# A spectral mixer and a gated unit on one core: the opening written out as one list of pieces, and scales from exponents and norms

## The chip, the cores and the metric

One NeuronCore of a Trainium2 chip. The time is the device time of one execution in microseconds; three executions of the kernel before gave 475.52, 474.89 and 474.98, median 474.98 us.

## The reference, cut to what matters

```python
def reference(A_x, A_w_r, A_w_i, B_x, B_W_gate, B_W_up, B_W_down):
    x = A_x                                   # 1 x 2048 x 448, float32
    xn = _layernorm(x, axis=-1)
    X = rfft2(xn, axes=(-2, -1)) * (A_w_r + 1j * A_w_i)
    a = irfft2(X, s=(2048, 448), axes=(-2, -1))
    gate, up = xn @ B_W_gate, xn @ B_W_up     # 448 x 1792 each
    b = ((gate * (gate > 0)) * up) @ B_W_down # 1792 x 448
    return x + a + b
```

## The kernel before, in words

The gated unit is done in float16 with every operand split in a high half and a low half (high = the value rounded to float16, low = the rest), so a product is three passes: high times high, high times low, low times high. Weights are first multiplied by a power of two so that the halves fit float16; these scales are found on the chip.

**Tiles.** x has 16 tiles n2 = 0..15 of 128 rows by 448. They form four chunks q = n2 mod 4, taken in the order `CHUNKS` = 0, 2, 1, 3; chunk 0 is the tiles 0, 4, 8, 12 and chunk 2 the tiles 2, 6, 10, 14. A chunk's normalized rows, transposed, are the tile `T` (`T_62` is chunk 0, `T_63` chunk 2). The 14 blocks of 128 columns of the gate and up weights are f = 0..13, in groups of 5, 5 and 4. The weights of one f come as two slabs `wst` of 256 KB, g = 0 (gate) and g = 1 (up).

**Units.** One unit is a pair (f, q): 20 matmuls of 512 columns into PSUM `gu` (`gu_full`, L653), 10 for each g, and its share of the half passes (`gu_half`, L660): a set of four matmuls of 64 rows that serves two units at once, the pair in `mates`. It closes one unit and opens the next. `gu` has two buffers. Then `gu_post` (L685 to L689): relu on ScalarE, product on VectorE, high half `h` on ScalarE, low half on VectorE. After the units of a group and chunk come four down projections (`dn_mm`, L702), each of 3 passes per f, that need `h` and the split down weights `wdt`.

**Normalization of a tile.** `ln_stats` (VectorE, L217, L220), `ln_rstd` (a square root on ScalarE and six small VectorE operations, L229 to L235), `ln_xn` (L253 or L255), `ln_hi` (ScalarE, L262 or L264, followed by two small copies on POOL, L265 and L266), `ln_lo` (VectorE, L276 and L277). Chunk 0 is then transposed by TensorE into PSUM (`ln_tp`, L290) and copied to `T` (`ln_ev`, L296 and L298); the other chunks by DMA transposes (`ln_dma`, L284).

**Scales.** Of the gate and up weights: `w_sq` squares a slab on ScalarE with a running sum (L590), POOL sums over the partitions (L593), `w_scale` makes four small VectorE operations (L601 to L605), `w_hl` the high half on ScalarE (L612) and the low half on VectorE (L613). Of the down weights: `wd_max`, a maximum on VectorE for each f (L618) and a maximum over the partitions on POOL (L620). Of the filter: `wmax_red`, 16 maxima on VectorE (L422).

**Order.** Up to the first unit the order on TensorE, VectorE, ScalarE and SyncE (which issues the DMAs) is written out by hand inside `manual_schedule` (L913 to L982), with `NWARM` = 24 and later a few matmuls on the tile `warm` that compute nothing. From the second unit on, a loop over the units (L1019) emits a unit, the pieces that `sched` has put at it, and as much of the list `bg` (the work of the Fourier transforms and of later chunks) as its planned share of VectorE allows (`room`, `load`); a scheduler then places each instruction on its engine's queue. Every engine works its own queue in order.

Of the kernel before, what the change touches and what calls it, by code (L numbers as in the profile page):

```python
# [134 lines left out]
def tile_gfnet_reglu(ctx: ExitStack, tc: tile.TileContext, x, xr, wgu, wd, wf, ident, c_fd, c_fm, c_im, c_row, c_id,  # L135
# [88 lines left out]
    def ln_rstd(q, js=(0, 1, 2, 3)):  # L224
        n = len(js)
        w = ft([128, 6, 4], F32, "rs", 3)
        vv, r0, t, r, nm, sd = (w[:, i, 0:n] for i in range(6))
# [20 lines left out]
    def ln_xn(n2, act=True):  # L248
        xn_b[n2] = free.pop(0)
        xn[n2] = xn_b[n2].rearrange("p g c k -> p (g c k)")[:, 0:D]  # L250
        r, nm = rst[n2 % 4, n2 // 4]
# [4 lines left out]

    def ln_hi(n2, fused=False):
        t = tt[n2]
        o = t.rearrange("p a b -> p (a b)")[:, 0:D]
        r, nm = rst[n2 % 4, n2 // 4]  # L260
        if fused:
            A.activation(o, xr_t[n2], AF.Identity, scale=r, bias=nm)  # L262
        else:
# [4 lines left out]
    def ln_norm(n2):
        new_tt(n2)
        ln_xn(n2, False)  # L270
        ln_hi(n2)
        free.append(xr_b.pop(n2))
# [819 lines left out]
```

## Time and profile before

| | |
|---|---|
| median of three executions | 474.98 us |
| the profiled execution | 474.69 us |
| its span, first to last instruction | 472.9 us |
| TensorE busy | 457.6 us (97%), 2713 matmuls |
| VectorE busy | 391.4 us (83%) |
| ScalarE busy | 169.9 us (36%) |
| POOL busy | 34.5 us (7%) |

Busy time is a sum over stages. In a slice of the span, the granted clock of TensorE is given as a share of full speed; a matmul that runs at half the clock is just as busy. A timeline row gives the start, the time from the first start to the last end of the merged instructions, engine, line and operation, what it writes and reads, how many, and in brackets the idle time of the engine before it and whose end released it.

### The profile page before, as it was taken

What the parts mean: (1) busy time and instruction counts of PE and PEld (TensorE: products, weight loads), DVE (VectorE), ACT (ScalarE), POOL (GpSimd) and SP (SyncE); (2) the same over time, 40 slices, a digit from 0 to 9 for tenths busy, and PEclk for the clock granted to TensorE, in tenths of its full rate; (3) what the DMA queues carried; (4) which work ended last, traced back from release to release, by engine and by line L of the source; (5) the groups of instructions that cost most, each with busy time, mean ns of one, the idle gap of its engine ahead of it and who ended that gap; (6) DMA issues with size and microseconds to landing.
All of it is one profiled execution on the core that took longest, in us unless ns stands there. A gap on an engine that the chain in (4) does not pass through costs nothing.

```text
span 472.9 us, 7492 instructions
## 1 busy us (share of the span) xinstructions
PE 457.6 (97%) x2713; PEld 235.2 (50%) x2713; DVE 391.4 (83%) x952; ACT 169.9 (36%) x342; POOL 34.5 (7%) x68
## 2 busy tenths in 40 slices
PE   8578999999999999999999999999999999999996
PEld 4433455555455555544444444444455655655653
DVE  6779459787989799998999999997989978856652
ACT  5746224241434275232212133253254134244120
POOL 2104002000500021000000001100000000000000
PEclk9899999999999999999999999999999999999999
DMA  7999501601144524314111010010231201200212
GB/s 256 384 380 238 144 0 35 124 17 51 37 106 139 157 94 135 103 39 120 41 41 40 1 40 21 2 45 1 71 99 52 82 15 45 91 32 25 77 43 78
DMA packets 38397, 41.38 MB, mean 87 GB/s; under 512 B 16390, under 2 KB 34534, under 8 KB 38360
## 3 DMA queue, kind: packets, MB, share of 16 engines
q1 hardware_dynamic: 38360, 40.90, 28.3%
q8 instruction: 21, 0.34, 0.3%
q14 instruction: 16, 0.13, 0.1%
HBM read 30.34 MB, written 3.67 MB: 72 GB/s over the span
## 4 chain that ended last, share of the span: by engine, by line
PE 89%; DVE 3%; DMA 2%; POOL 1%; issue 1%; ACT 1%; SPq 1%; POOLq 0%; ACTq 0%
PE gu L653 48%; PE dn L702 26%; PE gu L660 3%; PE fx L569 3%; PE fx L310 3%; PE fx L541 2%; PE fx L349 2%; DMA wst<-in_wgu 2%; PE fx L351 1%; PE fx L353 1%; POOL tt L265 1%; DMA T<-tt 1%; ACT junk L590 1%; DVE wdm L618 0%; ACT wt L612 0%
## 5 line engine op out<-in xcount | busy, mean ns | idle before, releaser
L653 PE MATMUL gu<-T,wt 128*128 128x512 f16 (+1 forms) x1140 | 256.7, 377 | 5.1 <-DVE wsc L603 2.5
L653 PEld LDWEIGHTS <-wt 128*128 128x128 f16 x1140 | 110.3, 98 | 133.9 <-issue 12.3
L702 PE MATMUL dn<-wdt,h 128*128 128x448 f16 x672 | 135.0, 352 | 1.7 <-ACT wdt L639 0.9
L702 PEld LDWEIGHTS <-h 128*128 128x128 f16 x672 | 65.3, 98 | 62.7 <-issue 3.5
L685 ACT ACTIVATE g<-gu 128x512 f32<-128x512 f32 x56 | 33.2, 593 | 102.4 <-PE gu L660 61.9
L686 DVE SCALAR_TENSOR_TENSOR g<-gu,g 128x512 f32<-128x512 f32 x56 | 38.5, 688 | 29.6 <-ACT g L685 29.5
L688 ACT ACTIVATE h<-g 128x512 f16<-128x512 f32 x56 | 35.0, 625 | 35.8 <-DVE g L686 35.8
L689 DVE TENSOR_TENSOR h<-g,h 128x512 f16<-128x512 f32 x56 | 38.6, 689 | 8.5 <-ACT h L688 8.4
L708 DVE SCALAR_TENSOR_TENSOR xy<-dn,dsc,xy 128x448 f32<-128x448 f32 x48 | 32.3, 680 | 6.2 <-PE dn L702 5.9
L612 ACT ACTIVATE wt<-wst,wsc 128x512 f16<-128x512 f32 x28 | 18.8, 713 | 16.2 <-DVE wsc L604 16.2
L613 DVE SCALAR_TENSOR_TENSOR wt<-wst,wsc,wt 128x512 f16<-128x512 f32 x28 | 20.4, 751 | 2.4 <-ACT wt L612 2.4
L557 ACT ACTIVATE pgh<-pg 114x512 f16<-114x512 f32 x16 | 10.1, 628 | 33.8 <-DVE pg L555 24.7
L593 POOL PARTITION_ALL_REDUCE wm<-wm x15 | 10.2, 681 | 159.2 <-ACT junk L590 159.2
L660 PE MATMUL gu<-T,wt 64*128 64x512 f16 x112 | 17.0, 381 | 3.3 <-DVE wt L613 2.7
L590 ACT ACTIVATE junk<-wst 128x512 bf16<-128x512 f32 x28 | 17.5, 623 | 7.4 <-DMA wst<-in_wgu 7.2
L569 PE MATMUL fx<-idc_t,pgh 114*128 114x112 f16 (+1 forms) x192 | 16.4, 236 | 0.0
L525 ACT ACTIVATE vt<-y,fsc 128x456 f16<-128x456 f32 x16 | 10.7, 671 | 14.4 <-PE fx L541 10.0
L342 ACT ACTIVATE Xh<-X 128x456 f16<-128x456 f32 x16 | 9.2, 577 | 17.8 <-PE fx L353 9.7
L560 DVE TENSOR_TENSOR pgh<-pg,pgh 114x512 f16<-114x512 f32 x16 | 11.0, 690 | 4.8 <-ACT pgh L557 4.7
L452 ACT ACTIVATE wf<-wf 128x114 f32<-128x114 f32 x16 | 4.6, 294 | 27.2 <-DVE y L459 13.1
L310 PE MATMUL fx<-fd_t,T 128*128 128x114 f16 x192 | 14.2, 225 | 0.0
L363 DVE TENSOR_TENSOR y<-y,y 128x456 f32<-128x456 f32 x22 | 13.8, 629 | 0.3
(113 smaller groups left out, 481.5 us busy)
## 6 DMA issues: line engine op xcount, KB each, us to landing
wst<-in_wgu SPq DMA_DIRECT2D x28, 256.0 KB
wmx<-in_wf SPq DMA_DIRECT2D x16, 228.0 KB
wf<-in_wf SPq DMA_DIRECT2D x16, 228.0 KB
wf<-y SPq DMA_DIRECT2D x32, 112.2 KB
y<-in_xr SPq DMA_DIRECT2D x16, 224.0 KB
xy<-in_x SPq DMA_DIRECT2D x16, 224.0 KB
out<-xy SPq DMA_DIRECT2D x16, 224.0 KB
wdst<-in_wd SPq DMA_DIRECT2D x14, 224.0 KB
```

Of the source, the lines that this page charges most:

```text
L310: P.matmul(o, T[:, a, js], fd_t[:, fd_off[part]:fd_off[part] + (2 * GW if part in wide else GW)], start=first, stop=True, skip_group_check ...
L569: P.matmul(ps[:, o0:o1], h[:, a, i, :], idc_t[:, b, c0:c0 + o1 - o0], start=(j == 0 and i < 3), stop=True, skip_group_check=True)
L590: A.activation(mt([128, 512], BF16, "junk"), wst[f, g].rearrange("p a b -> p (a b)"), AF.Square, scale=SQ, accum_out=m[:, 0, g:g + 1])
L613: V.scalar_tensor_tensor(w[:, 4:8, :], st, sc, w[:, 0:4, :], op0=OP.mult, op1=OP.subtract)
L653: last["P"] = P.matmul(hps[f, q][:, g, cs], wt[f, g][:, a, :], Tq[q][:, b, cs], start=(start and i == 0), stop=(stop and i == len(seq) - 1 ...
L660: m = P.matmul(hps[f, q][:, g, 0:512], wt[f, g][rows, 7, :], Tq[q][rows, b, :], start=start, stop=not start).ins
L685: last["A"] = A.activation(g1, hps[f, q][:, 0, :], AF.Relu, scale=2.0 ** -22).ins
L686: last["V"] = V.scalar_tensor_tensor(g1, hps[f, q][:, 1, :], 2.0 ** -22, g1, op0=OP.mult, op1=OP.mult).ins
L688: A.activation(h[:, 0, :], g1, AF.Copy)
L689: V.tensor_tensor(h[:, 1, :], g1, h[:, 0, :], op=OP.subtract)
L702: last["P"] = P.matmul(ps[:, 0:D], ht[f, q][:, a, js], wdt[f][:, b, :], start=(i == 0), stop=(i == n - 1)).ins
L708: last["V"] = V.scalar_tensor_tensor(xy[:, n2, :], dps[n2][:, 0:D], dsc[:, g:g + 1], xy[:, n2, :], op0=OP.mult, op1=OP.add).ins
```

## The change

`OPENING` lists the pieces of the first five units (f = 0..4 of chunk 0), one name for each, and each engine takes its own in the order of the list; POOL is now among the engines whose order is written by hand. The list holds the loads (`lx` and `ly` are x, `lw` a slab, `lwd` the down weights, `lfd` the constant `fd_t`), the normalization of the chunks 0 and 2, the scales, the splits, the matmuls (`hh`, `lh`, `hl` the quarters of unit one; `gu1g0` and so on the slabs of the next units; `hp` the half passes), the relu, product and halves of the five units, and the split of the down weights of the first group. All other work is held behind the list's last instructions on VectorE, ScalarE and SyncE, and the loop over the units starts at the sixth. `kw` and `warm` are the matmuls that compute nothing, 19 and three sets of 1, 6 and 3.

Scales: the squares with a running sum are used for the down weights and the filter too (`squares`, on ScalarE), in place of the VectorE maxima; the power of two comes from the exponent bits of the sum of squares by two integer operations (`half_exponent`, `shift_exponent`), so `w_scale` has two VectorE operations instead of four, `wd_scale` ten instead of eight. `ln_rstd` has five or, for the chunks 2, 1 and 3, four operations; `ln_xn` is always on VectorE. The loads of x and of the filter move to later units; the filter's loads and squares are spread through the transforms of the chunks 2 and 1.

```diff
+OPENING = """
+lx0 lx4 lw lid lw lx8 lx12 lw lw lw lw lx2 lx10 lx6 lx14 lwd0 lwd1 lwd2 lwd3 lwd4 warm st0 st4 sqA rsA hi4
+xn4 xn0 wsqW0g0 cp4 st8 hi0 parW0g0 st12 wsqW0g1 cp0 tpA0 lo0 tpA4 kw1 wscW0g0 sqB tpB0 kw6 parW0g1 wsqW1g0
+rsB whiW0g0 vevB0 lo4 wsqW1g1 xn12 tpB4 kw3 hi8 parW1 wscW0g1 xn8 whiW0g1 cp8 vevA0 vevA4 hi12 tpA8 vevB4
+hh10 hh00 lo8 wsqW2g1 cp12 tpA12 hl00 lo12 aevA12 tpB8 aevA8 hl10 wloW0g0 lw aevB8 tpB12 wscW1 lh00 aevB12
+wloW0g1 lw lfd hh01 hh11 whiW1g0 st2 lh01 lh10 whiW1g1 hl01 wloW1g0 lw hl11 wsqW2g0 wloW1g1 lw ly0 ly4 ly8
+ly12 lh11 wsqW3g0 st10 parW2 hp0 st14 wsqW3g1 gu1g0 st6 wdq0 parW3 wscW2 sqC wscW3 whiW2g0 rsC gu1g1 re0
+wloW2g0 whiW3g1 tm0 whiW2g1 xn6 wsqW4g0 xn2 gu2g0 wloW2g1 hi2 re1 xn10 gh0 wloW3g1 whiW3g0 tm1 gu2g1 wdq1
+wloW3g0 hi10 xn14 lo2 hi14 hi6 cp14 hp2 wsqW4g1 cp2 lo6 gu3g0 cp10 dm2 lo14 re2 parW4 wdq2 cp6 wscW4 tm2
+whiW4g0 dm14 lo10 wdq4 gu3g1 wloW4g0 gh1 dm10 gl0 whiW4g1 gl1 dm6 gu4g0 re3 wloW4g1 wdq3 tm3 wdp gh3
+wdsc gh2 gu4g1 gl2 wdh1 wdh2 wdl1 wdh0 wdl2 hp4 gl3 re4 wdh3 tm4 wdl0 gh4 wdh4 gl4 wdl3 wdl4 lw lw lw
+lw lw lw
+"""
...
+    def squares(src, acc):
+        A.activation(mt([128, 512], BF16, "junk")[:, 0:src.shape[-1]], src, AF.Square, scale=SQ, accum_out=acc)
+
+    def half_exponent(e, s):
+        V.tensor_scalar(e.bitcast(U32), s.bitcast(U32), 1, EXPMASK, op0=OP.logical_shift_right, op1=OP.bitwise_and)
+
+    def shift_exponent(o, e, sign, n):
+
+        V.tensor_scalar(o.bitcast(U32), e.bitcast(U32), float(sign), n * EXPONE, op0=OP.mult, op1=OP.add)
...
-        V.tensor_scalar(sc[:, 0, 0:n], e, TINY * SQ * 2.0 ** -64, 2.0 ** 50 / SQ, op0=OP.max, op1=OP.mult)
-        V.reciprocal(sc[:, 1, 0:n], sc[:, 0, 0:n])
-        V.tensor_scalar(e, e, TINY * SQ * 2.0 ** -64, 2.0 ** 64 / SQ, op0=OP.max, op1=OP.mult)
+        half_exponent(e, state["wm", f][:, 1, gs[0]:gs[-1] + 1])
+        shift_exponent(sc[:, 0:len(gs)], e, -1, 188)
...
-            V.tensor_reduce(m[:, 0, i:i + 1], wdst[f], axis=AX.X, op=OP.max, apply_absolute_value=True)
+        squares(wdst[f], state["wdm"][:, 0, i:i + 1])
...
-        V.tensor_reduce(small[:, k2:k2 + 1], state["wmx", k2], axis=AX.XY, op=OP.max, apply_absolute_value=True)
+        squares(state["wsq", k2].rearrange("p a b -> p (a b)"), small[:, k2:k2 + 1])
...
     with tc.manual_schedule(engines={mybir.EngineType.PE, mybir.EngineType.DVE, mybir.EngineType.Activation,
-                                     mybir.EngineType.SP}):
+                                     mybir.EngineType.SP, mybir.EngineType.Pool}):
...
+        for name in OPENING.split():
+            pieces[name]()
+    state["opened"] = True
+    free.extend(xr_b.pop(n2) for n2 in list(xr_b))
+    for e in "SVA":
+        ctx.enter_context(tc.issue_after(last[e]))
...
-    for i, u in enumerate(units):
+    for i, u in list(enumerate(units))[len(groups[0]):]:
```

SyncE's queue behind the first eleven loads, before: x and the down weights stand ahead of most of the slabs (`wst`). `y` read from in_xr is x for the normalization, `xy` read from in_x is x for the sum at the end, `wdst` the down weights.

```order
L195 DMA wst<-in_wgu 128x512 x4
L183 DMA xy<-in_x 128x448 x4
L189 DMA y_74<-in_xr 128x448
L189 DMA y_75<-in_xr 128x448
L189 DMA y_76<-in_xr 128x448
L189 DMA y_77<-in_xr 128x448
L195 DMA wst<-in_wgu 128x512
L205 DMA wdst<-in_wd 128x448 x5
L988 DMA fd_t<-in_c_fd 128x1710
L183 DMA xy<-in_x 128x448 x4
L209 DMA fm<-in_c_fm 128x768 x2
L195 DMA wst<-in_wgu 128x512
```

The same place in the changed kernel:

```order
L226 DMA wst<-in_wgu 128x512 x4
L220 DMA y_70<-in_xr 128x448
L220 DMA y_71<-in_xr 128x448
L220 DMA y_72<-in_xr 128x448
L220 DMA y_73<-in_xr 128x448
L236 DMA wdst<-in_wd 128x448 x5
L226 DMA wst<-in_wgu 128x512 x2
L976 DMA fd_t<-in_c_fd 128x1710
L226 DMA wst<-in_wgu 128x512 x2
L214 DMA xy<-in_x 128x448 x4
L319 DMA_TRANSPOSE T_63<-tt_97 128x8x128
```

The four slabs of the units four and five stand ahead of all loads of `xy`, and the transposes of chunk 2 right behind these.

POOL's queue from the fill of `warm`, before. `ISA` without operands configures POOL, `ISA wm<-wm` is the sum over the partitions, the copies are those of `ln_hi` for the x tiles `tt`:

```order
L925 MEMSET warm 128x512
L593 ISA
L593 ISA wm<-wm 128x1
L265 COPY tt_97<-tt_97 128x48
L266 COPY tt_97<-tt_97 128x64
L265 COPY tt_98<-tt_98 128x48
L266 COPY tt_98<-tt_98 128x64
L593 ISA wm<-wm 128x1
```

And in the changed kernel:

```order
L1031 MEMSET warm 128x512
L299 COPY tt_97<-tt_97 128x48
L300 COPY tt_97<-tt_97 128x64
L193 ISA
L193 ISA wm<-wm 128x1
L299 COPY tt_98<-tt_98 128x48
L300 COPY tt_98<-tt_98 128x64
L193 ISA wm<-wm 128x1
L193 ISA wm<-wm 128x2
```

The two copies of the first tile moved ahead of the configuring instruction.

VectorE's queue from the first normalization to the first low halves, before:

```order
L255 TENSOR_SCALAR y_70<-y_66,rs 128x448
L601 TENSOR_SCALAR eg<-wm 128x1
L603 TENSOR_SCALAR wsc<-eg 128x1
L604 RECIPROCAL wsc<-wsc 128x1
L605 TENSOR_SCALAR eg<-eg 128x1
L255 TENSOR_SCALAR y_71<-y_67,rs 128x448
L613 SCALAR_TENSOR_TENSOR wt<-wst,wsc,wt 128x512
L276 TENSOR_TENSOR tt_97<-y_70,tt_97 128x384
L277 TENSOR_TENSOR tt_97<-y_70,tt_97 128x64
L217 BN_STATS bst<-y_68 128x6
L220 BN_AGGR mv<-bst 128x2
```

And in the changed kernel:

```order
L286 TENSOR_SCALAR y_74<-y_67,mv,rs 128x448
L286 TENSOR_SCALAR y_75<-y_66,mv,rs 128x448
L248 BN_STATS bst<-y_68 128x6
L251 BN_AGGR mv<-bst 128x2
L248 BN_STATS bst<-y_69 128x6
L251 BN_AGGR mv<-bst 128x2
L310 TENSOR_TENSOR tt_98<-y_75,tt_98 128x384
L311 TENSOR_TENSOR tt_98<-y_75,tt_98 128x64
L196 TENSOR_SCALAR eg<-wm 128x1
L200 TENSOR_SCALAR wsc<-eg 128x1
L264 RECIPROCAL rs<-rs 128x2
```

Both statistics of the third and fourth tile moved ahead of the first scale, and the low half of the weights (`wt`) moved behind the low halves of all four tiles.

## Rows read from the trace of the kernel before

**Rows 1.** Busy time by stretch: stretch, length, TensorE, weight loads, VectorE, ScalarE, POOL, clock, DMA.
```profile
1.49:10.73 9.24, 9.09 (x35) 3.73 (x36) 6.43 (x22) 4.74 (x11) 1.77 (x5) 1.00 0.90 279
10.73:24.22 13.49, 8.55 (x70) 6.20 (x69) 10.19 (x35) 10.01 (x22) 2.68 (x7) 0.87 1.05 386
24.22:50.29 26.07, 21.67 (x105) 9.26 (x103) 21.89 (x64) 13.92 (x28) 6.39 (x11) 1.00 0.98 298
50.29:459.81 409.52, 409.48 (x2465) 211.74 (x2464) 348.84 (x825) 139.61 (x281) 22.71 (x36) 1.00 0.21 61
```

**Rows 2.** Timeline of TensorE in the first 51 us.
```profile
19.79 3.96 PE L653 MATMUL gu<-T,wt 128*128 128x256 f16 x20 [2.50 <-DVE wsc L603]
...
24.22 8.81 PE L653 MATMUL gu<-T,wt 128*128 128x512 f16 x40
35.75 0.61 PE L660 MATMUL gu<-T,wt 64*128 64x512 f16 x4 [2.72 <-DVE wt L613]
...
46.71 2.43 PE L702 MATMUL dn<-wdt,h 128*128 128x448 f16 x12 [0.23 <-DVE wdt L640]
49.75 0.61 PE L660 MATMUL gu<-T,wt 64*128 64x512 f16 x4 [0.61 <-DMA T<-tt]
```

**Rows 3.** The chain that ended last: start, length, what.
```profile
28.02 4.79 DMA wst<-in_wgu
...
57.81 4.32 PE gu L653 x20
...
200.75 5.67 PE dn L702 x30
```

**Rows 4.** VectorE: timeline rows, then groups by form (busy us, mean ns, idle before).
```profile
22.22 1.42 DVE L613 SCALAR_TENSOR_TENSOR wt<-wst,wsc,wt 128x512 f16<-128x512 f32 x2 [0.42 <-ACT wt L612]
...
37.03 1.35 DVE L255 TENSOR_SCALAR y<-y,rs 128x448 f32<-128x448 f32 x3
...
41.38 0.56 DVE L276 TENSOR_TENSOR tt<-y,tt 128x384 f16<-128x384 f32 x1
...
41.99 0.56 DVE L276 TENSOR_TENSOR tt<-y,tt 128x384 f16<-128x384 f32 x1
...
L422 DVE TENSOR_REDUCE small<-wmx 128x1 f32<-128x456 f32 x16 | 9.9, 626 | 3.8 <-DMA wmx<-in_wf 3.6
L217 DVE BATCH_NORM_STATS2 bst<-y 128x6 f32<-128x448 f32 x16 | 9.4, 617 | 2.5 <-DMA y<-in_xr 2.5
...
L234 DVE SCALAR_TENSOR_TENSOR rs<-rs 128x2 f32<-128x2 f32 x2 | 0.3, 161 | 0.1
```

**Rows 5.** ScalarE: two timeline rows, then the squares by form.
```profile
9.59 1.09 ACT L296 ACTIVATE T<-fx 128x384 f16<-128x384 f16 x2 [0.95 <-PE fx L290]
...
19.64 1.32 ACT L612 ACTIVATE wt<-wst,wsc 128x512 f16<-128x512 f32 x2
...
L590 ACT ACTIVATE junk<-wst 128x512 bf16<-128x512 f32 x28 | 17.5, 623 | 7.4 <-DMA wst<-in_wgu 7.2
...
L590 ACT ACTIVATION_READ_ACCUMULATOR junk<-wst 128x1 f32 x28 | 5.3, 188 | 0.0
```

**Rows 6.** Timeline of POOL: the first sum, copies of two x tiles.
```profile
6.30 0.53 POOL L593 PARTITION_ALL_REDUCE wm<-wm  x1 [4.87 <-ACT junk L590]
7.11 0.22 POOL L265 COPY tt<-tt 128x48 f16<-128x48 f16 x1 [0.27 <-ACT tt L262]
...
40.16 2.60 POOL L265 COPY tt<-tt 128x48 f16<-128x48 f16 x1
...
42.71 1.40 POOL L266 COPY tt<-tt 128x64 f16<-128x64 f16 x1
```

**Rows 7.** The transposes of chunk 2: SyncE's issue (timeline), transfer (chain).
```profile
41.63 6.06 SPq L284 DMA_TRANSPOSE T<-tt  x4
...
46.43 3.19 DMA T<-tt
```

More of the change, by code (lines that the diff above doesn't have):

```diff
@@ L268, in ln_norm @@
     def ln_norm(n2):
[L269 to L270 removed]
+        ln_xn(n2)
         ln_hi(n2)
+        ln_copy(n2)
         free.append(xr_b.pop(n2))
@@ L660, in gu_half @@
         m = P.matmul(hps[f, q][:, g, 0:512], wt[f, g][rows, 7, :], Tq[q][rows, b, :], start=start, stop=not start).ins
-        tc.add_manual_dep(m, prev.name, NOSYNC, reason="half passes stand together")
+        if "opened" in state:
+            tc.add_manual_dep(m, prev.name, NOSYNC, reason="half passes stand together")
         return m
@@ L726, in ln_chunk @@
     def ln_chunk(q):
-        if q != CHUNKS[1]:
-            for j in range(4):
-                add(0.0, load_xr, q + 4 * j)
+        for j in range(4):
+            add(0.0, load_xr, q + 4 * j)
         for j in range(4):
             add(0.79, ln_stats, q, j)
-        add(1.0, ln_rstd, q)
+        add(0.0, ln_sd, q)
+        add(0.7, ln_rstd, q)
         n = [q + 4 * j for j in (0, 2, 1, 3)]
@@ L752, in fft_chunk @@
                     add(0.0, load_fm, n[i])
+            k = state.get("wk", 0)
+            if q != CHUNKS[0] and k < 16:
+                if k > 1:
+                    add(0.0, wsq, k - 2)
+                add(0.0, wsq_load, k)
+                state["wk"] = k + 1
         for par in range(2):
@@ L767, in tile_gfnet_reglu @@
     fft_chunk(1)
-    for k in range(16):
-        add(0.0, wmax, k)
-        if k >= 2:
-            add(0.62, wmax_red, k - 2)
-    add(0.62, wmax_red, 14)
-    add(0.62, wmax_red, 15)
-    add(0.1, wmax_fin)
+    for k in (14, 15):
+        add(0.0, wsq, k)
+    add(0.1, wsq_fin)
     fft_chunk(3)
-    add(0.3, wmax_scale)
+    add(0.8, wsq_scale)
     add(0.0, open_inv)
@@ L978, in tile_gfnet_reglu @@
-        w_hl(1, 0)
-        w_hl(1, 1)
-        gu_full(0, 0, (1,), half[1], False, False, seq1 + seq2)
-        for j in range(4):
-            load_xr(CHUNKS[1] + 4 * j)
-    ctx.enter_context(tc.issue_after(last["V"]))
-    for _ in range(4):
-        load_wn()
-    for f in groups[0]:
-        load_wd(f)
-    nc.sync.dma_start(fd_t, c_fd)
+        gu_open(0, q)
+        for name in OPENING.split():
+            pieces[name]()
+    state["opened"] = True
+    free.extend(xr_b.pop(n2) for n2 in list(xr_b))
```

316 lines of the change are left out of this document (161 added, 155 removed).

## The prediction

> **What bounds the kernel now.** I read the busy time by stretch first, then TensorE's own timeline of the first 51 us, then what fed it there. From 50.29 to 459.81 us TensorE is busy 409.48 of 409.52 us [rows 1]: nothing that happens in that stretch on another engine shortens the run, as long as it stays off TensorE's path. VectorE is at 348.84 of 409.52 us there, so it is close behind, but it is behind. What is not filled lies in front: from 10.73 to 24.22 us TensorE has 8.55 us of 13.49 and from 24.22 to 50.29 us 21.67 of 26.07 [rows 1]. The timeline says where: 2.50 us of idle before the row at 19.79, 2.72 us before 35.75, 0.61 us before 49.75, and smaller ones around the first down passes at 46 us [rows 2]. The row at 19.79 is also slow: 20 narrow matmuls in 3.96 us, in a stretch with a granted clock of 0.87 [rows 1, 2]. Behind the wait at 35.75 stands a weight transfer of 4.79 us in the chain [rows 3], in a stretch in which the DMA engines are busy at 0.98 to 1.05 of their time [rows 1]; behind 49.75 the transposes of the second chunk [rows 7].
>
> **The frame of the sum.** After 50.29 us (the end of the half passes that close unit five and open unit six) the work of TensorE is the same list in both kernels. Before, 14 passes of the first down projection had been done by then (the 12 at 46.71 us and two just ahead of them [rows 2]); the new list ends with these half passes and does all down passes behind them. One pass is 5.67 / 30 = 0.189 us [rows 3], 14 are 2.65 us. So with H for the moment at which the half passes of unit five end,
> span after = H + (472.90 - 50.29) + 2.65 = H + 425.3.
> H in the terms of the kernel before is 50.29 - 2.65 = 47.6. The profiled execution took 474.69 us, 1.79 more than its span, and lies 0.29 under the median 474.98; I add both.
>
> **H, part by part: up to unit two.** The queue that is full first is VectorE's. The third and fourth tile of x are behind 1.47 MB of issued transfers, the same in both; before, 279 GB/s moved from 1.49 to 10.73 us, that is 2.58 MB, and then 386 GB/s [rows 1], so 1.47 MB is there about (2.58 - 1.47) / 0.386 = 2.9 us before 10.73: near 8 us. From 8.1 VectorE's list up to the second low half of unit one is: two statistics at 0.62 and a small operation of 0.16 each, 1.5; four low halves of x at the step of 0.61 from 41.38 to 41.99 [rows 4], 2.4; three scales of two small operations and one set of five, at 0.16 each or 0.2 with the hand-over [rows 4], 2.0; two normalizations at 1.35 / 3 = 0.45, 0.9; four copies out of PSUM, of 384 and 640 columns, for which I take 0.3 and 0.45 by their width against the 512 of a low half, 1.5; two low halves of weights at 1.42 / 2 = 0.71, 1.4 [rows 4]. Sum 9.7: it ends at 17.8. On the way, after the copy that frees the second PSUM buffer of the transposes (8.1 plus 6.8 of the above = 14.9), TensorE does six transposes and six narrow matmuls to 16.3; ScalarE then copies four T parts (0.49 to 0.7 each by 1.09 / 2 and width, 2.5 with a wait of 0.3 for the last transposes), makes two high halves of weights at 0.66 [rows 5], VectorE the low half, 0.75. That is 16.3 + 0.3 + 2.5 + 1.3 + 0.8 = 21.2, and the first half passes end at 21.8. Before they end at 24.22 [rows 2]: **2.4 us**.
>
> **Units two to five.** They hold 80 matmuls of 4.32 / 20 = 0.216 us [rows 3] and one more set of half passes, 50.29 - 49.75 = 0.54 us [rows 2]: 17.8 us, so 39.6 without a wait. Before, 26.07 us went there, 2.65 of them down passes; 4.40 us were idle [rows 1]. The waits go because of the transfers: the four slabs of units four and five come behind four tiles of x and wd alone (and fd_t between them), no longer behind twelve more tiles of x, fm and the x of a third chunk; each is issued when a low half frees its buffer, over 5 us ahead of its use. Five VectorE maxima of wd become ScalarE squares at 0.62 + 0.19 [rows 5]. What is late next is ScalarE: between 20.4 and 37 us its list has six high halves of weights (4.0), five squares of weights (3.8), four of wd (2.9), four high halves of x, three relus and two h copies (nine at 0.5 to 0.62, by width, 5.0), 15.7 of 16.6 us. So it is nearly full, and the last high half of weights is ready about when TensorE wants it. The last half passes need all four DMA transposes: before, four took 6.06 us of issue, some 1.4 apart, and the last landed at 46.43 + 3.19 = 49.6 [rows 7]. The new order can issue the first at 33 us, when the POOL copies are through, the last at 37; landing 3 us later, 40.2. **H = 40.2 + 0.6 = 40.8** if no operation slips. Two queues at 90% and more with in-order hand-overs don't run without a slip; I put 1.0 us on it, from the waits of 0.23 to 0.61 us that the same hand-overs show [rows 2]. H = 41.8, span 467.1, time 467.1 + 1.79 + 0.29 = **469.2 us**, 5.8 less than before (1.2%).
>
> **Edits that cost nothing here.** Sixteen maxima of the filter on VectorE at 0.626 [rows 4] become ScalarE squares; nine more wd maxima; scales of four operations become two; one operation less in each normalization set. That is some 18 us of VectorE after the opening; TensorE's 409.48 of 409.52 covers it all, so I count 0. The cover is TensorE itself: if it stood still for VectorE anywhere, part of it would count. ScalarE gets 25 x 0.81 = 20 us more on 139.61 us of 409.52 [rows 1]: it stays under half.
>
> **Where row and skill differ.** POOL's configuring instruction (the ISA row without operands) stood behind the memsets, its first use (6.30) waits 4.87 us for ScalarE [rows 6], so whatever it loads is hidden in at most these 4.87 us. In the new order it stands behind the first two copies, which end near 7.5, and its first use is wanted at 7.8. Its price lies between 0 and 4.87 us; I take a small one, since POOL starts its first use as soon as ScalarE is done. The Trainium skill, "GPSIMD Engine Reference", section 2.1 "Instruction dispatch", says that the first call to a freshly loaded kernel pays a load of about 6 us that no profile row shows. The row of 6.30 speaks against the full figure, since less time lay there; by the page's own 6 us H would be some 3.8 us later and the time 473.0.
>
> **Rivals.**
> 1. *The load of POOL comes out of cover.* With all of 4.87 us the first all-reduce is ready at 7.5 + 4.87 + 0.53 = 12.9; VectorE reaches the scale that needs it at 8.1 + 1.5 + 0.6 = 10.2 and stands 2.7 us, with everything queued behind it. Time 471.9. For it: no row shows the load. Against: nothing says it is as long as its cover. 0.11.
> 2. *The clock falls again.* Before, after the thin stretch to 19.79 us, 20 narrow matmuls and four half passes took 24.22 - 19.79 = 4.4 us, against 20 x 0.11 (half of 0.216) + 0.54 = 2.7 [rows 2, 3]. The new list has 10 extra matmuls on warm in the gaps up to 14 us and TensorE still waits some 3 us there. +1.7: 470.9. 0.08.
> 3. *POOL's copies of the second chunk starve.* Two copies take 0.22 each when free [rows 6], but 2.60 and 1.40 at 40.16, where VectorE runs two-input operations back to back [rows 4, 6]. I counted 0.9 per pair; three pairs stand in POOL's queue ahead of the sum for unit five's weights. At 2.0 per pair H is 3.3 later: 472.5. The Trainium skill, same page, section 8 "Key points", names this sharing of the SBUF interfaces for VectorE operations with two SBUF inputs; the rows agree. 0.08.
> 4. *Slower.* The 16 filter squares stand in ScalarE's order between the relus that free PSUM for TensorE, with two buffers, so a square waits for a load that waits for the square two before. A relu may be late by a unit of TensorE less relu and product, two operations of 512 columns (1.3 us by their width), so by 4.32 - 1.3 = 3.0 us, before TensorE stops. If 14 squares each wait as long as the longest load in the chain, 4.79 us [rows 3], 14 x (4.79 + 0.81 - 3.0) = 36 us are lost, 505 us; it is slower than before from 0.42 us per square on. Against: the DMA engines are at 0.21 after 50 us [rows 1]. 0.04.
> 5. *No change.* The gain is given back in the middle because VectorE's 85% there hides a bound: 475. 0.03.
>
> **How the numbers follow.** The forecast has 0.66, with H between 39.7 (TensorE without a wait) and 43: 467.1 to 470.4. The range takes in rivals 1 and 2 and most of 3: 467.0 to 472.5. About 0.2% (1 us) is what a measurement tells from no change here. Faster by more: 0.66 + 0.11 + 0.08 + 0.08 = 0.93; within 0.2% 0.03; slower 0.04.
>
> **What would show it.** TensorE's first half passes end near 22 us and those of unit five near 42; no idle over 1 us between; full clock in the opening; the stretch behind is still filled, 422 to 426 us long. If POOL's first all-reduce starts over 1 us after its square, rival 1 holds; if a row of matmuls after 15 us runs at half speed, rival 2; copies over 1 us near 32 us, rival 3; idle TensorE behind a relu near 60 to 170 us, rival 4. The forecast is wrong if H is over 44 or TensorE waits over 1 us in all behind it.

## The result and the profile after

The changed kernel takes 466.49 us (median of 466.03, 466.41, 466.57 and 466.72) against 474.94 us for the kernel before: 0.9818 of its time, 95% interval 0.9801 to 0.9835. That is 8.45 us faster. The prediction was 469.2 us with a range of 467.0 to 472.5: the direction and the place of the gain are right, the size is not, and the time lies 0.5 us under the low end of the range. The profiled execution took 466.57 us with a span of 464.8 us.

The page after: busy time, then the span in 40 slices (busy tenths, the granted clock of TensorE, the share of the DMA engines).

```profile
PE 455.4 (98%) x2714; PEld 234.0 (50%) x2714; DVE 374.1 (80%) x893; ACT 185.5 (40%) x402; POOL 28.0 (6%) x68
...
PEclk9999999999999999999999999999999999999999
DMA  7749957240711342230110100021110211200112
```

VectorE has 17.3 us less than before, ScalarE 15.6 us more, and no slice shows a lower clock; before, one did (the second of the 40, at 8 tenths). By stretch, from the first transposes to the first half passes, from there to the half passes of unit five, and behind them (columns as in [rows 1]):

```profile
8.36:20.32 11.96, 9.63 (x87) 6.53 (x87) 11.49 (x37) 9.36 (x21) 2.79 (x9) 1.00 0.80 281
20.32:39.27 18.95, 18.71 (x90) 7.82 (x89) 17.11 (x50) 16.46 (x39) 3.32 (x11) 1.00 0.62 167
39.27:464.80 425.53, 420.90 (x2523) 217.35 (x2521) 342.22 (x795) 155.83 (x337) 20.20 (x36) 1.00 0.26 78
```

In the 18.95 us of the units two to five TensorE is busy for 18.71; before, the corresponding stretch had 4.40 us of idle [rows 1]. TensorE's timeline of the opening, which answers to [rows 2]:

```profile
14.08 0.33 PE L325 MATMUL fx<-id_t,tt 128*128 128x128 f16 x3 [0.49 <-ACT wt L639]
...
16.59 3.01 PE L689 MATMUL gu<-T,wt 128*128 128x256 f16 x26
19.78 0.60 PE L696 MATMUL gu<-T,wt 64*128 64x512 f16 x4 [0.18 <-DVE wt L643]
...
25.05 4.48 PE L689 MATMUL gu<-T,wt 128*128 128x512 f16 x20 [0.24 <-DVE g L730]
29.46 0.60 PE L696 MATMUL gu<-T,wt 64*128 64x512 f16 x4
29.99 8.81 PE L689 MATMUL gu<-T,wt 128*128 128x512 f16 x40
38.73 0.60 PE L696 MATMUL gu<-T,wt 64*128 64x512 f16 x4
```

Read it against [rows 2]: the 20 narrow matmuls that took 3.96 us are part of a row of 26 in 3.01 us; the waits of 2.72 and 0.61 us ahead of the half passes are gone; the first half passes end at 20.32 us (24.22 before), those of unit five, the moment H of the prediction, at 39.27 us (47.6 before in the same terms). So 3.9 us came from the stretch up to the first half passes and 4.4 us from the units two to five. What is behind H takes 464.8 - 39.27 = 425.5 us; of the 4.6 us in it without work for TensorE 0.35 are one wait at 84.86 and 4.3 lie at the very end of the run, as many as before. VectorE's last three copies out of PSUM just ahead of the row at 14.08, from its timeline and from the view of the tile `fx` (shortest, median and longest in ns, first and last start):

```profile
13.59 1.01 DVE L333 COPY T<-fx 128x384 f16<-128x384 f16 x3
...
L333 DVE COPY T<-fx x3: 345/350/477, 13.6 to 14.1; 128x384 f16<-128x384 f16 x2, 128x640 f16<-128x640 f16 x1
```

The first of them, of tile 0, ends at 13.59 + 0.35 = 13.94, the last, of tile 4, at 14.60.

### The profile page after: what moved, and what is told of

Its sections match the earlier page's. It is cut to its first block, busy times and chain, and to the rows that moved or that the text cites. A ratio compares the mean times of both kernels' runs of the same rounds, so it can differ in the third digit from the quotient of the medians.

```text
span 464.8 us, 7505 instructions
## 1 busy us (share of the span) xinstructions
PE 455.4 (98%) x2714; PEld 234.0 (50%) x2714; DVE 374.1 (80%) x893; ACT 185.5 (40%) x402; POOL 28.0 (6%) x68
## 4 chain that ended last, share of the span: by engine, by line
PE 81%; issue 9%; DVE 3%; DMA 2%; ACT 1%; SPq 1%; POOL 1%; POOLq 0%; ACTq 0%
PE gu L689 43%; PE dn L757 25%; PE fx L607 3%; PE gu L696 3%; PE fx L579 2%; PE fx L384 2%; PE fx L345 2%; DMA wmx<-in_wf 1%; DMA y<-in_xr 1%; PE fx L386 1%; PE fx L388 1%; SPq L319 1%; POOL tt L300 0%; DVE y L286 0%; ACT junk L190 0%
## 5 line engine op out<-in xcount | busy, mean ns | idle before, releaser
L689 PE MATMUL gu<-T,wt 128*128 128x512 f16 (+1 forms) x1140 | 253.7, 375 | 0.2 <-DVE g L730 0.2
L607 PEld LDWEIGHTS <-pgh 114*128 114x128 f16 x192 | 13.7, 98 | 2.3 <-issue 0.4
L612 DVE SCALAR_TENSOR_TENSOR xy<-fx,fsc,xy 128x448 f32<-128x448 f32 x16 | 10.8, 678 | 4.6 <-PE fx L607 4.6
L399 DVE TENSOR_TENSOR y<-y,y 128x456 f32<-128x456 f32 x22 | 13.8, 628 | 0.5
L398 DVE TENSOR_TENSOR y<-y,y 128x456 f32<-128x456 f32 x22 | 13.8, 627 | 0.2
L579 PEld LDWEIGHTS <-vt 128*128 128x128 f16 x192 | 11.9, 98 | 3.8 <-issue 0.8
```

The costliest lines, as they stand in the source:

```text
L579: P.matmul(o, v[:, h, w], m[:, c, :], start=(i == 0), stop=(i == 2), skip_group_check=True)
L607: P.matmul(ps[:, o0:o1], h[:, a, i, :], idc_t[:, b, c0:c0 + o1 - o0], start=(j == 0 and i < 3), stop=True, skip_group_check=True)
L689: last["P"] = P.matmul(hps[f, q][:, g, cs], wt[f, g][:, a, :], Tq[q][:, b, cs], start=(start and i == 0), stop=(stop and i == len(seq) - 1 ...
```

## The experiments

Every kernel was timed beside the kernel before. Ten of the twelve are the changed kernel with one part altered (two in the last); two are the kernel before with one part added. Of the long lines of `OPENING` the diffs show the piece that changes. The kernel before took 474.94, 475.50, 475.12 and 475.15 us (medians) in the four sets of runs, so half a microsecond between two kernels of different sets tells nothing, and each timeline is that of one execution. For the opening one number is therefore used beside the times: from the moment at which VectorE begins the statistics of the third tile of x to the end of the first half passes. It is 12.00 us in the changed kernel, 20.32 - 8.32; VectorE's row there is

```profile
8.32 0.63 DVE L248 BATCH_NORM_STATS2 bst<-y 128x6 f32<-128x448 f32 x1 [1.22 <-DMA y<-in_xr]
```

### What sets the first half passes: three runs

**The first two tiles change places in TensorE's queue.**

```diff
-cp0 tpA0 lo0 tpA4 kw1
+cp0 tpA4 lo0 tpA0 kw1
```

> The transposes of the tiles 4 and 0 change places in TensorE's queue, so the third tile gets the PSUM buffer of tile 4 and has to wait for the second copy of tile 4 out of it, as the prediction had taken it for the changed kernel as it stands. Theory: the prediction's step failed there; with the swap the transposes of the third tile start at 14.7 instead of 14.1 and everything behind follows, first half passes 20.9 (0.6 later), time 467.1. Rival: the hand-over of that buffer isn't on the path (ScalarE's queue of copies and high halves is), first half passes within 0.2 us of 20.3, time 466.5.

Measured 466.75 us (466.13 to 467.13), first half passes at 20.30 us, 12.01 after the statistics at 8.29. The rival's number, but not for its reason. The third tile's transposes started at 14.06, as before the swap, while VectorE's three copies out of PSUM ran from 13.57 to 14.58; so they waited for the first copy at most (13.57 + 0.35 = 13.92), and the swap never made them wait for the last one. Why the buffer handed on is that of tile 0 in both orders, no row shows. The run says nothing on what a later hand-over costs. The next one does.

**The copies out of PSUM come later in VectorE's queue.**

```diff
-hi8 parW1 wscW0g1 xn8 whiW0g1 cp8 vevA0 vevA4 hi12 tpA8 vevB4
+hi8 parW1 wscW0g1 xn8 whiW0g1 cp8 lo8 vevA0 vevA4 hi12 tpA8 vevB4
...
-hh10 hh00 lo8 wsqW2g1
+hh10 hh00 wsqW2g1
```

> On VectorE the low half of the third tile (0.7 us) moves ahead of the three copies out of PSUM; nothing else moves. In every kernel with the new opening so far the first half passes ended 12.0 us after VectorE began the statistics of the third tile (20.32 after 8.32; 19.22 after 7.21; 20.30 after 8.29), whichever way round the first two tiles were transposed. Theory: the first copy (it ends at 13.94, TensorE goes on at 14.08) is the gate, and TensorE is filled from there to the half passes, so they end 12.5 to 12.7 us after the statistics, the time is 467.0. Rival: ScalarE's four copies of T set the half passes and not the gate; still 12.0 us.

Measured 467.05 us (466.72 to 467.67). The timelines of VectorE and TensorE in this kernel:

```profile
14.35 1.01 DVE L333 COPY T<-fx 128x384 f16<-128x384 f16 x3
...
14.85 0.33 PE L325 MATMUL fx<-id_t,tt 128*128 128x128 f16 x3 [1.29 <-DVE T L333]
...
20.54 0.60 PE L696 MATMUL gu<-T,wt 64*128 64x512 f16 x4 [0.27 <-DVE wt L643]
```

The copies begin at 14.35 in place of 13.59, TensorE goes on at 14.85 in place of 14.08, the first half passes end at 21.08, 12.80 us after the statistics at 8.28. The gate, that is the event that lets TensorE go on, moved by 0.8 us and the half passes by 0.8 us (0.1 more than the theory's 12.7): it is the first of the three copies, whose last was still running when TensorE went on, and TensorE's list behind it is filled. The row at 14.08 of the changed kernel names ScalarE's high half, since that ended 0.06 us after the copy; here, where it had long ended, the row names the copy.

**The third and fourth tile of x first.**

```diff
-lx0 lx4 lw lid lw lx8 lx12 lw lw lw lw
+lx0 lx4 lid lx8 lx12 lw lw lw lw lw lw
```

> The third and fourth tile of x are loaded ahead of the first two slabs of weights; nothing else moves on any engine. Theory: VectorE's list from the statistics of the third tile on, which waited 1.22 us for that load (8.32), sets the first half passes, by way of the scale of the up weights and ScalarE's queue; it starts at 7.1, ScalarE catches up with it at 12.45 instead of 13.28, so first half passes 19.5 (0.8 earlier) and the time 465.7. Rival: TensorE's transposes and buffers or ScalarE alone set it; then within 0.2 us of 20.3 and 466.5.

Measured 466.17 us (465.70 to 466.39); the statistics begin at 7.03, the first half passes end at 19.74, those of unit five at 38.52. The theory holds in part: 0.6 us of the 1.3 us by which VectorE began earlier arrive. The rest is mostly a new wait, 0.54 us of VectorE for the high half of the first tile:

```profile
9.14 0.56 DVE L310 TENSOR_TENSOR tt<-y,tt 128x384 f16<-128x384 f32 x1 [0.54 <-ACT tt L293]
```

ScalarE did it behind a square of weights that itself waited 0.67 us for its slab. The times of the two kernels overlap. The last experiment takes this wait away.

### The loads: what took the waits of the units two to five away

```diff
-lwd4 warm
+lwd4 ly0 ly4 ly8 ly12 lfd ly2 ly10 ly6 ly14 warm
...
-wloW0g1 lw lfd hh01
+wloW0g1 lw hh01
...
-wloW1g1 lw ly0 ly4 ly8
-ly12 lh11
+wloW1g1 lw
+lh11
...
-        for j in range(4):
+        for j in range(4 if c else 0):
```

> In the changed kernel eight tiles of x for the sum and the constant fd_t (2.28 MB) are loaded ahead of the four slabs of the units four and five, as they were before; the second four of them come there from a later unit. Theory: the early slabs are what took TensorE's waits of 2.72 and 0.61 us away; at 386 GB/s these transfers take 5.9 us, the slabs land 4.1 us later (24.6 for the first), ScalarE's squares of them stand and hold its queue for some 3 us, and the half passes of unit five end 2 to 4 us later: 468.5 to 470.5. Rival: the order on VectorE and ScalarE did it and the slabs had room, under 0.5 us later: 466.5 to 467.

Measured 472.95 us (471.67 to 473.27), ratio to the kernel before 0.9942 (0.9922 to 0.9962): 6.5 us of the 8.45 are gone, more than the theory's 4. ScalarE and TensorE, then two stretches of TensorE by windows:

```profile
24.83 0.63 ACT L190 ACTIVATE junk<-wst 128x512 bf16<-128x512 f32 x1 [5.52 <-DMA wst<-in_wgu]
...
29.32 6.64 PE L689 MATMUL gu<-T,wt 128*128 128x512 f16 x20 [4.69 <-DVE g L730]
...
24.63:29.32 4.69, 0.00 (x0) 0.10 (x1) 2.33 (x9) 4.43 (x11) 0.41 (x1) 0.74 0.04 16
29.32:35.90 6.58, 6.58 (x21) 2.37 (x21) 6.01 (x13) 5.67 (x14) 1.56 (x6) 0.66 0.00 1
```

The first slab arrives at 24.83, as worked out (24.6). ScalarE, in order, stands 5.52 us for it; the relu and the high halves that TensorE needs are behind it, and TensorE stands 4.69 us (0.24 in the changed kernel). Then comes what the expectation had not counted: the granted clock is 0.66, and 20 matmuls take 6.64 in place of 4.48 us, 2.2 us more. The half passes of unit five end at 45.71, 6.4 later. So without the order of the loads most of the gain doesn't exist. The order of this run is not quite the old one: before, the first of the four slabs stood behind four of the eight tiles, the last two behind still more than these eight.

### The clock: two runs

**The fillers left out of the new opening.**

```diff
-lo0 tpA4 kw1 wscW0g0 sqB tpB0 kw6 parW0g1
+lo0 tpA4 wscW0g0 sqB tpB0 parW0g1
...
-tpB4 kw3 hi8
+tpB4 hi8
```

> The ten matmuls on warm in the gaps of the opening (the sets of 1, 6 and 3) are left out. If they are what kept the granted clock of TensorE at full speed, the clock falls somewhere between 12 and 24 us as in the kernel before, some 20 to 30 narrow matmuls go at half speed, and the first half passes end 1.5 to 3 us later: 468 to 469.5. If the shorter gaps alone kept it (rival), the row of 26 narrow matmuls still takes 3.0 us and the time is 466.5.

Measured 467.65 us (467.00 to 468.75), 1.2 us more. The narrow matmuls and the stretch by windows:

```profile
14.61 1.06 PE L689 MATMUL gu<-T,wt 128*128 128x256 f16 x4
...
13.41:17.38 3.97, 3.97 (x30) 3.36 (x31) 3.90 (x12) 2.76 (x6) 0.60 (x2) 0.59 0.61 226
```

Four narrow matmuls take 1.06 us where they took 0.60; the granted clock is 0.59 for 4 us, and the half passes end 13.34 us after the statistics, 1.34 later than 12.00. The ten matmuls that compute nothing pay this back. The theory's mechanism shows, a little smaller than its 1.5 to 3 us: 14 narrow matmuls and 16 transposes fall into the slow stretch, not 20 to 30 narrow matmuls.

**Fillers in the kernel before, alone.**

```diff
+        keep_warm(9)
         gu_full(0, 0, (0,), half[0], False, False, seq2)
...
+        keep_warm(10)
         gu_full(0, 0, (0,), half[1], False, False, seq1 + seq2)
```

> The kernel before with 19 matmuls that compute nothing in TensorE's two gaps at 12.1 and 17.3 us; nothing else. The clock no longer falls behind the second gap, so 20 narrow matmuls take 2.3 in place of 3.96 us and the first half passes end 1.6 us earlier, at 22.6. Theory: the slab of unit four sets what comes then (it stands in the chain with 4.79 us), so the gain is waited away at 35.75 and the time stays at 474.9, within 0.4. Rival: the prediction's way of adding the parts also holds one by one, 473.3.

Measured 475.93 us (475.50 to 476.79), ratio 1.0022 (1.0008 to 1.0036): slower by 0.8 to 1 us. TensorE's timeline:

```profile
19.31 2.35 PE L653 MATMUL gu<-T,wt 128*128 128x256 f16 x20
21.59 0.60 PE L660 MATMUL gu<-T,wt 64*128 64x512 f16 x4
...
35.73 1.03 PE L660 MATMUL gu<-T,wt 64*128 64x512 f16 x4 [4.80 <-DVE wt L613]
36.70 10.50 PE L653 MATMUL gu<-T,wt 128*128 128x512 f16 x40
```

The 20 narrow matmuls take 2.35 us in place of 3.96 and the first half passes end 2.1 us earlier. All of it is waited away: the second half passes start at 35.73, in the kernel before at 35.75 [rows 2], after 4.80 us of idle in place of 2.72. Behind this longer idle time the clock is down (0.80 from 35.73 to 47.04 us), and 40 matmuls take 10.50 in place of 8.81 us. The theory holds in that a slab sets what comes then, and the price behind it was new. But the slab is not one of unit four. It is the first of unit five, the ninth that ScalarE squares, and it holds unit four up by the order on ScalarE. In the kernel before, two pieces of the chain and VectorE's row for unit four:

```profile
32.91 0.72 ACT junk L590 x2
33.63 0.49 ACT wt L612
...
34.28 1.42 DVE L613 SCALAR_TENSOR_TENSOR wt<-wst,wsc,wt 128x512 f16<-128x512 f32 x2 [1.25 <-ACT wt L612]
```

The transfer that began at 28.02 [rows 3] is for the square at 32.91. The high halves of unit four (L612) stand behind this square, and the low halves that TensorE waits for at 35.75 stand behind them. Their own scale was there at 32.0, so some 1.5 of the 2.72 us are the slab's; the rest is VectorE, which comes to that scale late, behind five maxima of down weights and other work. In the run with fillers the scale was there at 31.0, the square came at 32.02 and the high halves at 33.41.

### The scales: four runs

**The new scales in the kernel before.** The functions of the changed kernel for squares, exponents and norms replace the old ones, and with them the times that the plan for `bg` gives them; the opening and the place of the filter's loads stay.

```diff
-            V.tensor_reduce(m[:, 0, i:i + 1], wdst[f], axis=AX.X, op=OP.max, apply_absolute_value=True)
+            squares(wdst[f], m[:, 0, i:i + 1])
...
-        V.tensor_reduce(small[:, k2:k2 + 1], state["wmx", k2], axis=AX.XY, op=OP.max, apply_absolute_value=True)
+        squares(state["wmx", k2].rearrange("p a b -> p (a b)"), small[:, k2:k2 + 1])
```

> The kernel before with the scales of the changed kernel (squares on ScalarE for the down weights and the filter, scales from exponents with fewer VectorE operations) and the old opening. Theory: the opening made the gain; the waits for slabs and transposes are in the order of the loads, so the time is 474.9 within 0.7 (VectorE is some 18 us less busy, the idle of TensorE at 35.75 stays over 2 us). Rival: the lighter VectorE gets to its low halves earlier and so gives back slab buffers earlier; then 472 to 474.

Measured 481.44 us (480.06 to 482.37), ratio 1.0128 (1.0100 to 1.0155): 6.3 us slower, outside both expectations. VectorE is 14.9 us less busy, as meant. TensorE's half passes of unit five end at 51.03 (50.29 before): no gain there, three waits of 0.86, 1.13 and 1.72 us in place of the old ones. That the idle of 2.72 us at 35.75 would stay was wrong: the half passes of unit four now run without a wait.

```profile
32.39 0.60 PE L673 MATMUL gu<-T,wt 64*128 64x512 f16 x4
...
39.79 5.96 PE L666 MATMUL gu<-T,wt 128*128 128x512 f16 x19 [1.13 <-DVE wt L624]
```

Without the maxima VectorE has the scale of unit four at 28.4 in place of 32.0, so its high halves (28.46) come ahead of the square of unit five's first slab (33.36) and its low halves at 29.48 in place of 34.28, as the rival had it. The slab itself lands no earlier, so the wait comes back one unit later, as the 0.86 and 1.13 us for the weights of unit five, and with it a lower clock (0.71 from 39.79 to 45.63 us). The rest of the loss is far behind the opening. TensorE's rows there, and what the filter's squares waited for:

```profile
162.65 0.75 PE L364 MATMUL fx<-Xh,fm 128*128 128x456 f16 x3 [1.82 <-DMA fm<-in_c_fm]
165.89 0.74 PE L364 MATMUL fx<-Xh,fm 128*128 128x456 f16 x3 [0.81 <-DVE y L415]
170.57 0.91 PE L325 MATMUL fx<-fd_t,T 128*128 128x114 f16 x12 [1.61 <-ACT y L409]
177.09 0.92 PE L325 MATMUL fx<-fd_t,T 128*128 128x114 f16 x12 [0.97 <-DVE eo L346]
...
  DMA wmx<-in_wf: 11.0, 11
```

The old order has the 16 pieces of the filter in a row. On VectorE that was harmless; on ScalarE each square waits for its load in front of the relus and copies of everybody else, 11.0 us in 11 waits, and TensorE stands 5.2 us. The first of these waits (1.82) goes another way: it is for `fm`, a constant of the transforms, whose load stands in SyncE's queue behind loads of the filter, and SyncE waited 9.1 us in all, from 125 to 180 us, for squares to give buffers back. This is the mechanism of rival 4 of the prediction, at work in another kernel, though it is transforms that it holds up: none of the four waits names a relu.

**The filter in a row in the changed kernel.**

```diff
-            k = state.get("wk", 0)
-            if q != CHUNKS[0] and k < 16:
-                if k > 1:
-                    add(0.0, wsq, k - 2)
-                add(0.0, wsq_load, k)
-                state["wk"] = k + 1
...
+    for k in range(16):
+        add(0.0, wsq_load, k)
+        if k >= 2:
+            add(0.0, wsq, k - 2)
```

> The changed kernel with the loads and squares of the filter in one row behind the transforms of the third chunk, as the old order had the maxima, in place of spread through the transforms of two chunks. With the new scales in the kernel before, which had them in a row, ScalarE waited 11.0 us for 11 of these loads near 141 to 168 us, and TensorE 5.2 us behind it. Theory: the spreading of these loads is what keeps this cost away, so it comes back here: TensorE waits 4 to 6 us near 150 us and the time is 470.5 to 472.5. Rival: the wait came from other work in the old order (its transfers), and the time stays at 466.5 within 0.7.

Measured 471.05 us (470.24 to 472.81), ratio 0.9918 (0.9891 to 0.9945): 4.6 us of the gain gone. TensorE's rows, the squares' wait, one stretch by windows:

```profile
138.18 0.75 PE L384 MATMUL fx<-Xh,fm 128*128 128x456 f16 x3 [0.34 <-DMA fm<-in_c_fm]
140.64 0.37 PE L384 MATMUL fx<-Xh,fm 128*128 128x456 f16 x1 [1.10 <-DMA fm<-in_c_fm]
148.26 1.32 PE L345 MATMUL fx<-fd_t,T 128*128 128x114 f16 x12 [2.12 <-DVE y L435]
...
  DMA wmx<-in_wf: 10.2, 12
...
148.26:152.00 3.74, 3.73 (x20) 2.07 (x21) 3.65 (x10) 2.66 (x8) 0.97 (x2) 0.55 0.01 2
```

TensorE waits 3.6 us, a little less than the 4 to 6 expected (1.44 of them for `fm` again), and the clock is 0.55 behind it. The theory holds: the change keeps rival 4 away by spreading these loads. In the changed kernel ScalarE waits 10.0 us for the filter, too, but in 4 waits between 66 and 127 us, and TensorE's only wait between 40 and 450 us is one of 0.35 us at 84.86.

**The filter's maxima on VectorE in the changed kernel.**

```diff
-        squares(state["wsq", k2].rearrange("p a b -> p (a b)"), small[:, k2:k2 + 1])
+        V.tensor_reduce(small[:, k2:k2 + 1], state["wsq", k2], axis=AX.XY, op=OP.max, apply_absolute_value=True)
```

> The changed kernel with the filter's 16 maxima on VectorE again, in place of 16 squares on ScalarE: 16 x 0.626 = 10.0 us more VectorE work, all of it behind the opening. Theory: TensorE covers it, 466.5 within 0.5. Rival: VectorE is so close behind TensorE in the middle that part of its saving of 17 us made the gain that the prediction's sum lacks; then 468 or more, with TensorE waiting for VectorE between 60 and 250 us.

Measured 466.01 us (464.90 to 466.27), against 466.49: no loss. The 10 us of VectorE that moved to ScalarE behind the opening bought nothing, as the prediction had counted them.

**The old scales of the weights in the new opening.**

```diff
-        half_exponent(e, state["wm", f][:, 1, gs[0]:gs[-1] + 1])
-        shift_exponent(sc[:, 0:len(gs)], e, -1, 188)
+        V.tensor_scalar(e.bitcast(U32), m[:, 1, g].bitcast(U32), 1, EXPMASK, op0=OP.logical_shift_right,
+                        op1=OP.bitwise_and)
+        V.tensor_scalar(sc[:, 0, 0:n], e, TINY * SQ * 2.0 ** -64, 2.0 ** 50 / SQ, op0=OP.max, op1=OP.mult)
+        V.reciprocal(sc[:, 1, 0:n], sc[:, 0, 0:n])
+        V.tensor_scalar(e, e, TINY * SQ * 2.0 ** -64, 2.0 ** 64 / SQ, op0=OP.max, op1=OP.mult)
...
-        squares(wdst[f], state["wdm"][:, 0, i:i + 1])
+        V.tensor_reduce(state["wdm"][:, 0, i:i + 1], wdst[f], axis=AX.X, op=OP.max, apply_absolute_value=True)
```

> The changed kernel with the old scales of the weights: four small VectorE operations in each scale in place of two, and the maxima of the down weights on VectorE (5 x 0.61 in the opening) in place of squares on ScalarE. In the opening VectorE gets six scales x 0.4 and five maxima x 0.61, 5.4 us, between 8 and 37 us, where it has some 3 us of idle. Theory: the new opening needs the lighter scales in part: first half passes 0.8 later by two scales, those of unit five 2 to 3 us later, 468.5 to 469.5. Rival: the waits that the old opening had came from the loads alone and VectorE has room, under 0.7 us: 466.5 to 467.2.

Measured 468.04 us (467.81 to 468.29), 1.55 us more, between the two expectations and nearer the theory's. TensorE:

```profile
25.61 4.48 PE L697 MATMUL gu<-T,wt 128*128 128x512 f16 x20 [0.71 <-DVE g L738]
...
36.48 4.28 PE L697 MATMUL gu<-T,wt 128*128 128x512 f16 x19 [1.22 <-DVE wt L650]
```

The first half passes end 12.57 us after the statistics (7.84 to 20.41), 0.6 more than 12.00; the units two to five take 20.81 us, 1.9 more, in two waits for VectorE. Together that is 2.4 us, inside the theory's 2 to 3. In this execution the statistics began 0.5 us earlier than in the changed kernel, which hides part of it. Behind H it is 425.0 us (425.5), so the lighter scales count in the opening alone.

### The frame: one microsecond for one

```diff
-wsqW3g1 gu1g0
+wsqW3g1 kw10 gu1g0
```

> Ten matmuls of 512 columns that compute nothing stand in TensorE's queue right behind the first half passes, ahead of unit two: 10 x 0.216 = 2.2 us. Theory (the frame of the sum): what is behind unit five is one filled list of TensorE, so every microsecond by which the opening is longer counts in full: the half passes of unit five end 2.2 us later (41.4) and the time is 468.7. Rival: from unit two on VectorE, ScalarE or the transposes set the pace of the opening and TensorE only waits for them, or the middle has slack; then under 1 us of it is left, 467.4 or less.

Measured 467.57 us (466.74 to 467.76), 1.1 us more, where theory said 2.2 and the rival under 1. The execution profiled (466.74) was the fastest of the four:

```profile
19.22 2.33 PE L974 MATMUL dn<-warm 128*128 128x512 f16 x10
...
39.40 0.61 PE L696 MATMUL gu<-T,wt 64*128 64x512 f16 x4
```

In it the ten matmuls took 2.17 us (19.22 to 21.39). From the statistics (7.21) to the half passes of unit five (39.94) it is 32.73 us against 39.27 - 8.32 = 30.95, so 1.8 of the 2.17 us arrive there; the wait of 0.24 us for the product at 25 us is gone. Behind it the span has 425.0 us against 425.5; the wait of 0.35 us at 84.86 is not there, 0.2 us stay unexplained. So the frame holds for the part ahead of H to 0.4 us, but small waits later give some back; the ten kernels with the new opening and the filter's loads spread have 425.0 to 425.7 us behind H.

### A version that goes a little further

```diff
-lx0 lx4 lw lid lw lx8 lx12 lw lw lw lw
+lx0 lx4 lid lx8 lx12 lw lw lw lw lw lw
...
-xn4 xn0 wsqW0g0 cp4 st8 hi0 parW0g0 st12 wsqW0g1 cp0 tpA0
+xn4 xn0 hi0 cp4 st8 cp0 wsqW0g0 parW0g0 st12 wsqW0g1 tpA0
```

> As with x loaded first, and the high half of the first tile stands ahead of the first square of weights in ScalarE's queue (POOL's copies and TensorE's transposes of that tile follow it). With x first alone VectorE waited 0.54 us for that high half, behind a square that waited 0.67 us for its slab. Theory: this wait goes, VectorE's list runs through, first half passes at 19.1 to 19.2, those of unit five at 38.0, the time 465.4. Rival: another hand-over takes its place (the scale of the gate weights, now that their slab comes later), 466.2 as with x first alone.

Measured 465.71 us (465.23 to 466.24), ratio to the kernel before 0.9803 (0.9783 to 0.9822). The first half passes end at 19.28, those of unit five at 38.19, 1.1 us earlier than in the changed kernel and within 0.2 us of the theory; of the rival's kind there is one wait of VectorE, 0.16 us for POOL's sum. The times of the two differ by 0.8 us, and their intervals overlap; the timeline is the better witness here.

## Why the prediction was wrong, and where it was right

**Right: what bounds, and where the gain is.** TensorE is filled behind the opening (420.90 of 425.53 us, at full clock, and almost all of the rest lies at the very end) and the gain is in the opening; the order of the loads is what the units two to five needed (undone: 6.5 us lost; lighter scales alone moved the first of the two waits one unit on and didn't take it away); the 10 us of filter work are covered (put back: none lost). The stretch behind H was put at 425.3 us and is 425.5.

**Wrong: four terms, 2.7 us in all, three of them on the same side.**

- *First half passes at 21.8; they end at 20.32 (1.5).* The step that failed is "after the copy that frees the second PSUM buffer of the transposes (8.1 plus 6.8 of the above = 14.9), TensorE does six transposes". It took the fourth copy, that of tile 4, for the gate. The gate is the first of the last three, which ended at 13.94, and the copy of tile 4 ended 0.66 us later; the run with later copies shows that such a shift counts one for one. So 0.66 of the 1.5 us are this step. The rest are sizes: VectorE began 0.2 later (8.32) but needed 0.5 less than walked to the end of these copies, and TensorE and ScalarE behind the gate took 6.4 us in place of 6.9.
- *Units two to five at 20.0; they take 18.95 (1.05).* The step that failed is "I put 1.0 us on it", for slips of two nearly full queues: the only wait of TensorE in there is 0.24 us. Under it, two errors cancel, so that the 19.0 us without the slip come so near is luck. The half passes of units two to five are two sets, not one (29.46 and 38.73), and a matmul takes 4.41 / 20 = 0.22 us there, so TensorE alone needs 18.7 and not 17.8. And the transposes, which were to end the stretch at 40.2, did not: the half passes at 38.73 started without idle time.
- *The tail: 425.3 against 425.5 (0.2 the other way).*
- *Time from span: 1.79 + 0.29 against 1.77 - 0.08 (0.4).* The median was laid 0.29 above the profiled run because it had been so before; after, it lies 0.08 below.

The range failed for one reason: its low end was "TensorE without a wait", H at 39.7, counted from first half passes at 21.8 that had no lower bound of their own.

**The rivals.** *POOL's load* (rival 1) did not come. POOL's timeline, whose configuring instruction stands between the copies and the sum:

```profile
7.26 0.24 POOL L300 COPY tt<-tt 128x64 f16<-128x64 f16 x1
7.75 0.40 POOL L193 PARTITION_ALL_REDUCE wm<-wm  x1 [0.25 <-ACT junk L190]
```

The copy ends at 7.50 and the first sum starts 0.25 us later, when ScalarE's square is done. The Trainium skill, "GPSIMD Engine Reference", section 2.1 "Instruction dispatch", expects about 6 us for the first call of a kernel that was just loaded; nothing of that kind lies between these two rows, and the measurement decides. *The clock* (rival 2) stayed at 1.00, and the run without fillers shows that this was bought: left out, they cost 1.3 us against the 1.7 of the rival. *Starving copies* (rival 3) show in small:

```profile
30.40 0.22 POOL L299 COPY tt<-tt 128x48 f16<-128x48 f16 x1
30.56 0.59 POOL L300 COPY tt<-tt 128x64 f16<-128x64 f16 x1
...
30.50 0.56 DVE L310 TENSOR_TENSOR tt<-y,tt 128x384 f16<-128x384 f32 x1 [0.57 <-ACT tt L295]
```

A copy that takes 0.24 us free takes 0.59 beside a two-input operation of VectorE, far from the 2.60 of [rows 6]. The Trainium skill, "GPSIMD Engine Reference", section 8 "Key points", names a contention of the two engines for such operations with two inputs in SBUF; the rows agree. *Squares in ScalarE's order* (rival 4) did not come in the changed kernel, but two runs bring it out, at 3.6 and 5.2 us of TensorE's waits: the mechanism was right (behind transforms and `fm`, not behind a relu), and what keeps it away is the spreading of the loads, which the rival had not counted. *No change* (rival 5) fell with the filled middle.

**What the parts are worth.** Undone one at a time in the changed kernel: order of the loads 6.5 us, spread filter loads 4.6, lighter weight scales 1.55, fillers 1.2. That is more than the whole 8.45, and the two parts that were put into the kernel before alone made it slower, by 0.8 and 6.3 us. They aren't terms of a sum: each takes away the next wait that the others uncover. One part has no run of its own: of the 3.9 us up to the first half passes the fillers (1.34) and the lighter scales (0.6) were undone, but not the new order of VectorE, ScalarE and POOL; that the remaining 2 us or so are its worth is argued and not shown.

## What to carry to other kernels

Where a wait behind a load ends a stretch, nothing ahead of it counts until the load itself comes earlier; find that one first. Moving work to an idle engine is free only if what it waits for is free too: on an engine that works in order, a square that waits for its load stands in front of everybody's work, so spread the loads. When walking a hand-over of two buffers, find which copy frees the buffer, not just the last in the row, and give each moment that a range is built on a lower bound of its own.

## What the runs showed of the hardware that was not expected

- Idle time can cost twice. After 4.69 us of idle TensorE ran 20 matmuls at a granted clock of 0.66 (6.64 in place of 4.48 us); after 4.80 us 40 of them took 10.50 in place of 8.81; after 2.12 us, which followed waits of 0.34 and 1.10 us at 138 and 141 us, the clock was 0.55 for 3.7 us. These are means over a stretch: in shorter windows the rows read 0.50 (29.32 to 33 us of the run with the loads ahead), the lower of the clock's two levels (1.2 of 2.4 GHz), and then 1.00 (34 to 35.9). A single wait of 2.72 us behind a full stretch [rows 2] and one of 1.22 us in the run with the old weight scales had no such price.
- The third tile of x, loaded in the same order in nine of the eleven kernels with the new opening, let VectorE start between 7.21 and 8.32 us in the one profiled execution of each. That is 1.1 us that the order of the loads doesn't explain, and it passes straight to the first half passes (7.21 to 19.22, 8.32 to 20.32), so a gain or loss of that size in one timeline can be chance.
